# A top-k mask with the subtraction turned round, and a weight decode with its passes in another order

## The chip, the cores and the metric

The kernel runs on one core of one Trainium2 chip. The metric is the device time of one execution in microseconds. Before the change it is 1667.4 us, the median of three runs (1666.01 to 1667.79).

The core has five engines that run side by side and meet through semaphores: TensorE (PE, with weight loads shown as PEld), VectorE (DVE), ScalarE (ACT), GpSimd (POOL) and SyncE (SP), which here only issues DMAs. Each engine takes its instructions strictly in order, so an instruction that waits holds up everything behind it on that engine.

## The reference

Attention with a top-32 mask per query row, then a feed-forward block with an ELU.

```python
# q, k, v: (8, 8, 576, 64) float32
scores = scale * np.matmul(q, k.transpose(0, 1, 3, 2))
kth = np.partition(scores, -32, axis=-1)[..., -32:-31]
scores = np.where(scores >= kth, scores, -1e9)
scores = scores - np.max(scores, axis=-1, keepdims=True)
attn = np.exp(scores)
attn = attn / (np.sum(attn, axis=-1, keepdims=True) + 1e-09)
x = np.matmul(attn, v)                       # then (B,H,S,D) -> (4608, 512)
h = x @ w_in                                 # w_in  (512, 2048)
g = np.where(h > 0, h, np.exp(np.minimum(h, 0)) - 1)
out = g @ w_out                              # w_out (2048, 512)
```

The two weight matrices arrive as 64-bit floats. The kernel reads each weight as two 32-bit words and puts a 32-bit float together from them on the chip.

## The kernel before, in words

**Attention steps.** The queries are cut into tiles of 128 rows (and a rest of 64 per image). One `Step` is one tile with one pair of heads; there are 144. Per step, PE computes the scores of both heads into PSUM (`scores`, L299), ACT copies them to the tile `sc` (L307), and DVE finds the 32 largest values of each row: four rounds of an eight-wide maximum with a replace between them. The 32nd largest is the last column of `u.last` (`low` in `mask`), the largest the first column of `u.first` (`top`).

**Mask.** `mask(u, i)` takes one head of a step. POOL forms `neg = -low` (L366) and `gap = low - top` (L368), both 128x1. ACT then runs a leaky rectifier with bias `neg` in place (L369): scores from the 32nd up become `s - low`, the others are multiplied by 1e30. A second pass, the exponential with bias `gap` (L370), turns the kept ones into exp(s - top) and the others into 0, and adds up the row for the denominator. Then POOL forms the reciprocal and scales both heads (`normalise`, L380 to L387), PE transposes the result (`turn`, L406), ACT copies it out (L407), PE multiplies it with v (`attend`, L432) and ACT copies that to `xT` (L459).

**Feed-forward pieces.** `feed` hands out pieces of the feed-forward block between the parts of a step: `hidden` (PE L504, ACT L514, L517 and L519, DVE L476 for the ELU) and `project` (PE L529). A piece is only handed out once `decoded` says that the weights it needs have been through the decode.

**Decode.** There are 32 weight pieces of 128x512, 16 of `w_in` and 16 of `w_out`. `load_weight` brings one into a `raw` tile (SP queue, L153); `raw` has seven buffers. In that tile the low word (`lo`) and the high word (`hi`) of each weight alternate, so each is read and written at a stride of 8 bytes; `sign` is the top byte of the low word. `convert_first(i)` runs on ACT a Copy that scales the low word (L174), a Sign that writes the byte (L175) and an Abs that scales the high word in place (L178), and on POOL a clamp of the high word (L179). `convert_last(i)` shifts the high word on DVE (L186) and adds both words on POOL into the final weight tile (L187). `decode_piece(i)` does `convert_first(i)` and `convert_last(i - 3)`; it is called by `hook`, which the rounds of the selection call. Each of the first eight steps calls it four times, always in pairs, and step 8 three times, 35 calls in all.

**Order.** The first eight steps (`n < tight`) use `select_row` and `mask(cur, i)` on the step itself, and outside the first few lines of the start-up the order of instructions on each engine is worked out by the scheduler of the framework. From step 8 on the order is the written one: step n selects, while step n-1 is masked and step n-2 transposed.

Of the kernel before, what the change touches and what calls it, by code (L numbers as in the profile page):

```python
# [8 lines left out]
AF = mybir.ActivationFunctionType  # L9
ALU = mybir.AluOpType  # L10
FP32 = mybir.dt.float32
U32 = mybir.dt.uint32
I32 = mybir.dt.int32
# [3 lines left out]
TOP_K = 32  # L17
TAKEN = -1.0e30
EPS = 1.0e-9
STEEP = 1.0e30  # L20
HIDDEN = {1: 1.1, 2: 1.85, 3: 2.7}
PROJECT = 3.55

# [58 lines left out]
def kernel(  # L82
# [9 lines left out]
    nc = tc.nc  # L92
    P = nc.NUM_PARTITIONS
# [8 lines left out]
    NF = dff // P  # L102
# [3 lines left out]
    scale = 1.0 / float(D) ** 0.5  # L106
# [3 lines left out]
    def pool(name, bufs, **kw):  # L110
        return ctx.enter_context(tc.tile_pool(name=name, bufs=bufs, **kw))
# [7 lines left out]
    small = pool("small", 4)  # L119
# [20 lines left out]
    raw = {}  # L140

    def weight(i):
        per = dff // WN
        if i < NC * per:
            f, c = divmod(i, NC)
            src = moe_w_in[c * P : (c + 1) * P, 2 * f * WN : 2 * (f + 1) * WN]
            return src, w_in[:, c, f * WN : (f + 1) * WN]
        f = i - NC * per
        return moe_w_out[f * P : (f + 1) * P, :], w_out[:, f, :]

    def load_weight(i):
        t = rawpool.tile([P, 2 * WN], U32, tag="raw", name="raw")
        nc.sync.dma_start(t[:], weight(i)[0])  # L153
        raw[i] = t

    def parts(t):
        words = t[:].rearrange("p (n w) -> p n w", w=2)
        signs = t[:].bitcast(FP8).rearrange("p (n w) -> p n w", w=8)
        return words[:, :, 0], words[:, :, 1], signs[:, :, 3]

    def convert_first(i):

        lo, hi, sign = parts(raw[i])
        ef, mf = hi.bitcast(FP32), lo.bitcast(FP32)
        nc.scalar.activation(mf, lo, AF.Copy, scale=2.0**-35, bias=2.0**17)  # L174
        nc.scalar.activation(  # L175
            sign, ef, AF.Sign, scale=2.0**64, bias=1.0, saturate=False
        )
        nc.scalar.activation(ef, ef, AF.Abs, scale=2.0**-62)  # L178
        nc.gpsimd.tensor_scalar(  # L179
            ef, ef, (2.0 - 2.0**-3 - 2.0**-23) * 2.0**-46, 2.0**-77, ALU.min, ALU.max  # L180
        )

    def convert_last(i):
        t, dst = raw.pop(i), weight(i)[1]
        lo, hi, sign = parts(t)
        nc.vector.tensor_single_scalar(hi, hi, 3, ALU.logical_shift_left)  # L186
        nc.gpsimd.tensor_tensor(  # L187
            dst.bitcast(I32), hi.bitcast(I32), lo.bitcast(I32), ALU.add
        )

    decode = []
    decoded = [0]
# [10 lines left out]
            late["x"] = ctx.enter_context(tc.tile_pool(name="xt", bufs=2))  # L203

    def decode_piece(i):
        if i < 2 * NF:
            if i + 3 < 2 * NF:
                load_weight(i + 3)
            convert_first(i)
        if i > 2:  # L210
            convert_last(i - 3)
            decoded[0] = i - 2

    loaded, kqT, vT = {}, {}, {}

# [65 lines left out]
    def turn_qk(whole=False):  # L281
        while turning:
            if next(turning[0], turning) is turning:
                turning.pop(0)
            elif not whole:
                return
# [3 lines left out]
    def scores(u):  # L290

        u.sc = scpool.tile([P, 2, S], FP32, tag="sc", name="sc")
        q0 = QUERIES + u.t.qt * P
        for half in range(2):
            for h, i, rows in u.heads:
                kq = kqT[u.t.b, h // 2]
                part = slice(i * D, (i + 1) * D)
                k0 = (KEYS if i == 0 else 0) + half * HS
                nc.tensor.matmul(  # L299
                    wide[i][rows, half, 0:HS],  # L300
                    kq[part, q0 : q0 + u.t.ql],
                    kq[part, k0 : k0 + HS],
                    start=True,
                    stop=True,
                )
        for i in range(2):
            nc.scalar.activation(  # L307
                u.sc[:, i, :].rearrange("p (a s) -> p a s", a=2),
                wide[i][:, :, 0:HS], AF.Copy, scale=scale,
            )  # L310

    def select_row(u, i):
        if i == 0:
            u.first = small.tile([P, 2, 8], FP32, tag="m1", name="m1")
            u.last = small.tile([P, 2, 8], FP32, tag="m4", name="m4")
        sc = u.sc[:, i, :]
        m = u.first[:, i, :]
        nc.vector.max(m, sc)
        wk = wkpool.tile([P, S], FP32, tag=f"wk{i}", name="wk")
        cur = sc  # L320
        for r in range(TOP_K // 8 - 1):
            nc.vector.match_replace(wk[:], m, cur, TAKEN)
            cur = wk[:]
            if r < TOP_K // 8 - 2:
                m = small.tile([P, 8], FP32, tag=f"m{i}", name="m")[:]
            else:
                m = u.last[:, i, :]
            nc.vector.max(m, cur)
            if r > 0:
                hook()  # L330
            if r != 1:
                yield
# [21 lines left out]
            hook()  # L354
            yield

    def mask(u, i):

        if u.masked:
            return  # L360
        if i == 0:
            u.den = small.tile([P, 2], FP32, tag="den", name="den")
        u.masked = i == 1
        sc, low, top = u.sc[:, i, :], u.last[:, i, 7:8], u.first[:, i, 0:1]
        neg = small.tile([P, 1], FP32, tag="neg", name="neg")
        nc.gpsimd.tensor_scalar_mul(neg[:], low, -1.0)  # L366
        gap = small.tile([P, 1], FP32, tag="gap", name="gap")
        nc.gpsimd.tensor_tensor(gap[:], low, top, ALU.subtract)  # L368
        nc.scalar.activation(sc, sc, AF.Prelu, bias=neg[:], alpha=STEEP)  # L369
        nc.scalar.activation(  # L370
            sc, sc, AF.Exp, bias=gap[:], accum_out=u.den[:, i : i + 1]
        )

    def normalise(u):

        if u.normal:
            return
        u.normal = True
        den = small.tile([P, 2], FP32, tag="dene", name="dene")
        nc.gpsimd.tensor_scalar_add(den[:], u.den[:], EPS)  # L380
        rec = small.tile([P, 2], FP32, tag="rec", name="rec")
        nc.gpsimd.tensor_tensor(rec[:], den[:], power[:], ALU.pow)
        nc.gpsimd.tensor_tensor(den[:], den[:], rec[:], ALU.mult)
        nc.gpsimd.tensor_scalar(den[:], den[:], -1.0, 2.0, ALU.mult, ALU.add)
        nc.gpsimd.tensor_tensor(rec[:], rec[:], den[:], ALU.mult)
        for i in range(2):
            nc.gpsimd.tensor_scalar(  # L387
                u.sc[:, i, :], u.sc[:, i, :], rec[:, i : i + 1], 1.0, ALU.mult, ALU.mult
            )
# [168 lines left out]
    for b in range(B):  # L558
# [12 lines left out]
        for qt in range(J + 1):  # L571
# [8 lines left out]
            t = Tile(b, qt, rows, blk, slice(c0, c0 + n))  # L580
# [72 lines left out]
    def step(n):  # L653
        return steps[n] if 0 <= n < NS else None
# [3 lines left out]
    for n in range(NS + 3):  # L658
        for fn, args in todo.pop(n, []):
            fn(*args)  # L660
        ahead, cur, prev, done = step(n + 2), step(n), step(n - 1), step(n - 2)
        if n < tight:
            turn_qk(True)
            scores(ahead)
            for i in range(2):
                passes = select_row(cur, i)
                next(passes)
                if i == 0:
                    while closing:
                        attend(closing.pop(0))  # L670
                elif prev:
                    normalise(prev)
                    turn(prev, main)
                    turn(prev, rest)
                    turn(prev, other)
                feed(n, 0.25)
                next(passes)
                mask(cur, i)
                feed(n, 0.25)
            continue  # L680
        if n == tight:
            ctx.enter_context(tc.manual_schedule(engines=engines))
        passes = select(cur) if cur else iter(range(4))
        if ahead:
            scores(ahead)
        while closing:
            attend(closing.pop(0))
        next(passes)
        feed(n, 0.25)
        if prev:  # L690
            mask(prev, 0)
        turn_qk()
        next(passes)
        feed(n, 0.25)
        if done:
            turn(done, main)
            turn(done, rest)
        if prev:
            mask(prev, 1)
        next(passes)  # L700
        feed(n, 0.25)
        if done:
            turn(done, other)
        next(passes)
        if prev:
            normalise(prev)
        feed(n, 0.25)
        turn_qk(True)
# [36 lines left out]
```

## Time and profile before

| what | value |
|---|---|
| median of three runs | 1667.4 us |
| the profiled execution | 1667.02 us, its span 1665.2 us |
| PE busy | 1592.8 us, 96% of the span |
| DVE busy | 1495.8 us, 90% |
| ACT busy | 1165.1 us, 70% |
| POOL busy | 630.5 us, 38% |
| mean granted TensorE clock | 0.977 |

The shares are averages over parts of the run that differ. The decode falls into the first 150 us. In the 40 slices of the page, of 41.6 us each, PE is busy 5, 5, 8 and then 9 tenths for the rest, and the granted clock of TensorE reads 9, 5, 7, 8 and then 9. DVE's busy share falls off only in the last three slices.

### The profile page before, as it was taken

The numbers are of one execution on the slowest core, as the hardware profiler recorded it, in microseconds if no ns is written. First come the engines' busy times: TensorE is split into PE (matmuls) and PEld (weight loads), VectorE is DVE, ScalarE is ACT, GpSimd is POOL, SyncE is SP. The second block draws the span as 40 slices with busy tenths as digits, with TensorE's granted clock in tenths as the row PEclk, the third lists the DMA queues.
The fourth block names the chain that finished last, engine by engine and source line by source line (L and its number), as shares of the span: only waits on it lengthen the run. The fifth ranks groups of instructions, "written<-read, shape, count | busy, mean of one in ns | idle before, by whom it ended". The sixth has DMA issues, their size and how long they took to land.

```text
span 1665.2 us, 25986 instructions
## 1 busy us (share of the span) xinstructions
PE 1592.8 (96%) x8528; PEld 1031.5 (62%) x8528; DVE 1495.8 (90%) x3044; ACT 1165.1 (70%) x2377; POOL 630.5 (38%) x1719
## 2 busy tenths in 40 slices
PE   5589999999999999999999999999999999999999
PEld 3366677657574767656566676755557575755565
DVE  5887999999999999999999999999999999998500
ACT  6998777668686777678667685868758585857521
POOL 3775444333334334333334333333333343332200
PEclk9578999999999999999999999999999999999999
DMA  7540120001100110001100111001200100000000
GB/s 211 171 144 7 23 50 29 7 15 44 48 1 8 43 42 22 1 28 37 42 14 1 50 29 35 1 14 43 50 13 1 28 15 29 7 7 7 7 13 13
DMA packets 101126, 56.21 MB, mean 34 GB/s; under 512 B 84096, under 2 KB 92288, under 8 KB 100992
## 3 DMA queue, kind: packets, MB, share of 16 engines
q1 hardware_dynamic: 99792, 54.26, 11.7%
q8 instruction: 68, 1.11, 0.3%
q14 instruction: 66, 0.54, 0.1%
q10 hardware_dynamic: 1200, 0.30, 0.1%
HBM read 45.09 MB, written 9.44 MB: 33 GB/s over the span
## 4 chain that ended last, share of the span: by engine, by line
PE 65%; DVE 21%; ACT 9%; POOL 3%; issue 2%; SPq 0%; DMA 0%; ACTq 0%; POOLq 0%; DVEq 0%
PE ops L529 24%; PE hps L504 20%; DVE wk L346 9%; DVE m L353 8%; PE avps L432 7%; PE scps L299 6%; PE eps L406 5%; DVE m L341 3%; ACT sc L370 2%; ACT sc L369 1%; DVE gT L476 1%; ACT raw L175 1%; PE qkps L269 1%; ACT et L407 1%; POOL w_in L187 1%
## 5 line engine op out<-in xcount | busy, mean ns | idle before, releaser
L353 DVE MAX8 m<-wk 128x8 f32<-128x576 f32 x816 | 577.0, 750 | 0.0
L504 PE MATMUL hps<-xT,w_in 128*128 128x256 f32 (+2 forms) x2432 | 548.1, 374 | 12.5 <-ACT xT L459 12.3
L529 PE MATMUL ops<-w_out,gT 128*128 128x512 f32 x1152 | 522.8, 598 | 0.0
L504 PEld LDWEIGHTS hps<-xT,w_in 128*128 128x128 f32 x2432 | 406.5, 193 | 109.2 <-issue 23.8
L346 DVE MATCH_REPLACE8 wk<-m,wk 128x576 f32<-128x576 f32 x544 | 400.8, 746 | 0.0
L529 PEld LDWEIGHTS ops<-w_out,gT 128*128 128x128 f32 x1152 | 208.7, 190 | 233.0 <-issue 219.5
L380 POOL TENSOR_SCALAR dene<-den 128x2 f32<-128x2 f32 x144 | 35.9, 249 | 771.2 <-ACT sc L370 770.6
L369 ACT ACTIVATE sc<-sc,neg 128x576 f32<-128x576 f32 x288 | 226.8, 788 | 89.2 <-POOL neg L366 89.0
L370 ACT ACTIVATE sc<-sc,gap 128x576 f32<-128x576 f32 x288 | 224.1, 778 | 25.7 <-ACT sc L369 0.7
L387 POOL TENSOR_SCALAR sc<-sc,rec 128x576 f32<-128x576 f32 x288 | 221.0, 778 | 14.9
L307 ACT ACTIVATE sc<-scps 128x576 f32<-128x576 f32 x288 | 174.0, 659 | 73.3 <-PE scps L299 73.3
L299 PE MATMUL scps<-kqT 64*128 64x288 f32 (+1 forms) x1280 | 201.8, 440 | 21.2 <-ACT kqT L275 7.9
L407 ACT COPY et<-eps 128x512 f32<-128x512 f32 x288 | 166.8, 579 | 55.2 <-PE eps L406 55.0
L346 DVE MATCH_REPLACE8 wk<-m,sc 128x576 f32<-128x576 f32 x272 | 200.4, 746 | 0.0
L432 PE MATMUL avps<-et,vT 128*64 128x256 f32 (+2 forms) x2080 | 193.3, 326 | 4.8 <-ACT et L407 4.6
L406 PEld LDWEIGHTS eps<-ident,sc 128*128 128x128 f32 x1152 | 143.6, 144 | 83.8 <-issue 46.2
L476 DVE SCALAR_TENSOR_TENSOR gT<-n,gT 128x512 f32<-128x512 f32 (+1 forms) x132 | 100.2, 759 | 102.0 <-ACT n L519 101.9
L341 DVE MAX8 m<-sc 128x8 f32<-128x576 f32 x272 | 191.8, 748 | 0.0
L406 PE MATMUL eps<-ident,sc 128*128 128x128 f32 x1152 | 175.7, 278 | 15.4 <-POOL sc L387 13.0
L432 PEld LDWEIGHTS avps<-et,vT 128*64 128x64 f32 x2080 | 122.6, 141 | 79.1 <-issue 22.8
L299 PEld LDWEIGHTS scps<-kqT 64*128 64x128 f32 (+1 forms) x1280 | 108.1, 181 | 91.9 <-issue 44.2
L514 ACT ACTIVATE n<-hps 128x512 f32<-128x512 f32 (+1 forms) x156 | 88.0, 564 | 71.4 <-PE hps L504 67.5
(47 smaller groups left out, 1170.2 us busy)
## 6 DMA issues: line engine op xcount, KB each, us to landing
kin<-in_k_dram SPq DMA_DIRECT2D x64, 128.0 KB, 2.8
raw<-in_moe_w_in_dram SPq DMA_DIRECT2D x16, 512.0 KB, 5.4
vT<-in_v_dram SPq DMA_DIRECT2D x64, 128.0 KB, 2.3
raw<-in_moe_w_out_dram SPq DMA_DIRECT2D x16, 512.0 KB, 3.9
out_dram<-osb SPq DMA_DIRECT2D x32, 256.0 KB, 2.3
qin<-in_q_dram SPq DMA_DIRECT2D x62, 128.0 KB, 2.8
kin<-in_k_dram SPq DMA_DIRECT2D x32, 32.0 KB, 2.4
vT<-in_v_dram SPq DMA_DIRECT2D x64, 16.0 KB, 2.2
```

The costliest lines, as they stand in the source:

```text
L299: nc.tensor.matmul(wide[i][rows, half, 0:HS], kq[part, q0 : q0 + u.t.ql], kq[part, k0 : k0 + HS], start=True, stop=True,)
L341: nc.vector.max(found[i], cur[i])
L346: nc.vector.match_replace(wk[i], found[i], cur[i], TAKEN)
L353: nc.vector.max(found[i], cur[i])
L369: nc.scalar.activation(sc, sc, AF.Prelu, bias=neg[:], alpha=STEEP)
L370: nc.scalar.activation(sc, sc, AF.Exp, bias=gap[:], accum_out=u.den[:, i : i + 1])
L387: nc.gpsimd.tensor_scalar(u.sc[:, i, :], u.sc[:, i, :], rec[:, i : i + 1], 1.0, ALU.mult, ALU.mult)
L406: nc.tensor.transpose(ps[:, c * P : (c + 1) * P], sc[:, c0 : c0 + P], ident[:])
L407: nc.scalar.copy(g.et[:, chunks, u.at, :], ps[:, 0 : n * P].rearrange("p (c q) -> p c q", c=n),)
L432: nc.tensor.matmul(ps[i * D : (i + 1) * D, cols], vt[:, 2 * J + i if c == J else i * J + c, :], w, start=(c == 0), stop=(c == J),)
L504: nc.tensor.matmul(blk.h[:, f % bank, :], w_in[:, i, f * P : (f + 1) * P], blk.xT[:, i, 0:n_tok], start=(i == 0), stop=(i == NC - 1),)
L529: nc.tensor.matmul(blk.o[:], blk.gT[f // NG][:, f % NG, s * P : (s + 1) * P], w_out[:, f, :], start=(f == 0), stop=(f == NF - 1),)
```

## The change

Five edits:

1. `mask` no longer forms `neg`. The rectifier gets scale -1 and bias `low`, so that it works on `low - s`: the scores that fall out stay as they are, the kept ones are multiplied by 2^-96. The exponential gets scale -2^96, which undoes that for the kept ones and sends the others to 0.
2. `gap` is formed on DVE in the first eight steps and on POOL after that, as before.
3. Of the three ACT passes of a weight piece, Abs comes first and writes into the final weight tile instead of in place; Copy follows.
4. The POOL clamp (now in the final tile) and the Sign pass move one call of `decode_piece` later.
5. The DVE shift works in the final tile, one call earlier than before relative to the last add; the add is in place in the final tile.

```diff
-STEEP = 1.0e30
+STEEP = 2.0**96
...
-        lo, hi, sign = parts(raw[i])
-        ef, mf = hi.bitcast(FP32), lo.bitcast(FP32)
-        nc.scalar.activation(mf, lo, AF.Copy, scale=2.0**-35, bias=2.0**17)
+        lo, hi, _ = parts(raw[i])
+        nc.scalar.activation(weight(i)[1], hi.bitcast(FP32), AF.Abs, scale=2.0**-62)
+        nc.scalar.activation(lo.bitcast(FP32), lo, AF.Copy, scale=2.0**-35, bias=2.0**17)
+
+    def convert_second(i):
+        _, hi, sign = parts(raw[i])
+        w = weight(i)[1]
+        nc.gpsimd.tensor_scalar(
+            w, w, (2.0 - 2.0**-3 - 2.0**-23) * 2.0**-46, 2.0**-77, ALU.min, ALU.max
+        )
         nc.scalar.activation(
-            sign, ef, AF.Sign, scale=2.0**64, bias=1.0, saturate=False
+            sign, hi.bitcast(FP32), AF.Sign, scale=2.0**64, bias=1.0, saturate=False
         )
-        nc.scalar.activation(ef, ef, AF.Abs, scale=2.0**-62)
-        nc.gpsimd.tensor_scalar(
-            ef, ef, (2.0 - 2.0**-3 - 2.0**-23) * 2.0**-46, 2.0**-77, ALU.min, ALU.max
-        )
+
+    def convert_third(i):
+        w = weight(i)[1].bitcast(U32)
+        nc.vector.tensor_single_scalar(w, w, 3, ALU.logical_shift_left)
 
     def convert_last(i):
-        t, dst = raw.pop(i), weight(i)[1]
-        lo, hi, sign = parts(t)
-        nc.vector.tensor_single_scalar(hi, hi, 3, ALU.logical_shift_left)
-        nc.gpsimd.tensor_tensor(
-            dst.bitcast(I32), hi.bitcast(I32), lo.bitcast(I32), ALU.add
-        )
+        w, t = weight(i)[1].bitcast(I32), raw.pop(i)
+        nc.gpsimd.tensor_tensor(w, w, parts(t)[0].bitcast(I32), ALU.add)
...
     def decode_piece(i):
-        if i < 2 * NF:
-            if i + 3 < 2 * NF:
-                load_weight(i + 3)
-            convert_first(i)
-        if i > 2:
-            convert_last(i - 3)
-            decoded[0] = i - 2
+        stages = (convert_first, convert_second, convert_third, convert_last)
+        if i + 3 < 2 * NF:
+            load_weight(i + 3)
+        for ago, stage in enumerate(stages):
+            if 0 <= i - ago < 2 * NF:
+                stage(i - ago)
+        decoded[0] = max(0, i - 2)
...
-    def mask(u, i):
+    def mask(u, i, engine=nc.gpsimd):
...
-        neg = small.tile([P, 1], FP32, tag="neg", name="neg")
-        nc.gpsimd.tensor_scalar_mul(neg[:], low, -1.0)
         gap = small.tile([P, 1], FP32, tag="gap", name="gap")
-        nc.gpsimd.tensor_tensor(gap[:], low, top, ALU.subtract)
-        nc.scalar.activation(sc, sc, AF.Prelu, bias=neg[:], alpha=STEEP)
+        engine.tensor_tensor(gap[:], low, top, ALU.subtract)
+        nc.scalar.activation(sc, sc, AF.Prelu, scale=-1.0, bias=low, alpha=1.0 / STEEP)
         nc.scalar.activation(
-            sc, sc, AF.Exp, bias=gap[:], accum_out=u.den[:, i : i + 1]
+            sc, sc, AF.Exp, scale=-STEEP, bias=gap[:], accum_out=u.den[:, i : i + 1]
         )
...
-                mask(cur, i)
+                mask(cur, i, nc.vector)
```

## The prediction

> **What bounds the kernel now.** I read four views in this order: the busy time by stretch of the span, the groups of ACT in the decode, ACT's instructions in order of time there, and the list of who waited for whom. The columns of the first are the stretch, its length, then busy time (and instructions) of PE, PEld, DVE, ACT and POOL, the granted clock, the DMA share and GB/s.
>
> ```profile
> 13.00:40.00 27.00, 20.59 (x100) 13.86 (x96) 21.43 (x45) 21.32 (x40) 9.17 (x22) 0.94 0.75 227
> 40.00:145.00 105.00, 71.69 (x355) 52.76 (x356) 78.78 (x162) 103.02 (x175) 74.05 (x124) 0.66 0.41 126
> 145.00:300.00 155.00, 152.94 (x1192) 110.72 (x1191) 155.00 (x321) 111.74 (x238) 65.37 (x184) 1.00 0.11 29
> 300.00:600.00 300.00, 289.25 (x1568) 195.19 (x1567) 300.00 (x615) 220.01 (x459) 114.83 (x331) 1.00 0.10 26
> 600.00:1666.00 1066.00, 1055.58 (x5309) 656.67 (x5307) 940.12 (x1903) 704.03 (x1460) 364.73 (x1048) 1.00 0.08 21
> ```
>
> There are three stages with three limits. From 40 to 145 us ACT is busy 103.0 of 105.0 us while PE and DVE have 33 and 26 us to spare: ACT sets the pace. From 145 to 600 us DVE has no idle time at all (455.00 of 455). After 600 us PE is busy 1055.6 of 1066. Each stage hands over to the next, and the orders are fixed, so a microsecond saved in the first stage moves the end by about one. A microsecond saved on POOL or ACT after 145 us is worth nothing unless DVE or PE waited for it.
>
> What fills ACT in the first stage (13 to 145 us):
>
> ```profile
> L175 ACT ACTIVATE raw<-raw 128x512 fp8e4<-128x512 f32 x31 | 39.8, 1418 | 0.1
> L178 ACT ACTIVATE raw<-raw 128x512 f32<-128x512 f32 x31 | 20.6, 737 | 0.1
> L174 ACT ACTIVATE raw<-raw 128x512 f32<-128x512 uint32 x31 | 20.4, 731 | 0.7 <-DMA raw<-in_moe_w_in_dram 0.7
> L307 ACT ACTIVATE sc<-scps 128x576 f32<-128x576 f32 x22 | 14.6, 683 | 4.4 <-PE scps L299 4.4
> ```
>
> The decode is 80.8 us of ACT. Sign alone is half: its mean is 1418 ns against 731 and 737. The change keeps all three passes, so the bulk stays. The question is what of ACT's order and of its waits changes. ACT in order of time (start, length, line; in brackets the idle time before it and who ended it):
>
> ```profile
> 9.33 1.33 ACT L175 ACTIVATE raw<-raw 128x512 fp8e4<-128x512 f32 x1
> 10.42 0.35 ACT L261 COPY kqT<-scps 128x128 f32<-128x128 f32 x1
> ...
> 13.75 1.34 ACT L175 ACTIVATE raw<-raw 128x512 fp8e4<-128x512 f32 x1
> ...
> 15.67 1.17 ACT L307 ACTIVATE sc<-scps 128x576 f32<-128x576 f32 x2
> ...
> 83.02 2.51 ACT L175 ACTIVATE raw<-raw 128x512 fp8e4<-128x512 f32 x2
> 85.24 1.31 ACT L178 ACTIVATE raw<-raw 128x512 f32<-128x512 f32 x2
> 86.40 0.80 ACT L369 ACTIVATE sc<-sc,neg 128x576 f32<-128x576 f32 x1
> 87.82 0.58 ACT L407 COPY et<-eps 128x512 f32<-128x512 f32 x1 [0.63 <-PE eps L406]
> ...
> 104.89 0.71 ACT L519 ACTIVATE n<-n 128x512 f32<-128x512 f32 x1
> 105.41 1.34 ACT L174 ACTIVATE raw<-raw 128x512 f32<-128x512 uint32 x2
> ```
>
> ACT runs one pass right behind another. Of the instructions that end an idle time from 40 us on, only three are over a tenth: 0.70 (at 57.9), 0.65 (at 72.9) and 0.63 us, all the copy of the transposed scores, which waits for PE, which waits for POOL's scaling. The whole run's waits say the same of the mask:
>
> ```profile
> ACT sc L369 <- POOL neg L366: 89.0, 72, 4.5
> POOL neg L366 <- DVE m L353: 63.1, 80, 3.0
> DVE raw L186 <- POOL raw L179: 38.3, 19, 12.2
> ```
>
> The rectifier's wait of 89 us looks large, but most of it is a wait for the selection itself (POOL's `neg` waits 63 us for DVE's last maximum), and nearly all falls after 145 us, where ACT is idle a fourth of the time. It isn't 89 us to be had.
>
> **The change part by part.**
>
> The mask. Removed: 288 POOL instructions `neg`, median 0.22 us, 63 us of POOL. POOL is busy 38%, so that buys nothing by itself. ACT's two passes stay at 0.8 us each: scale and alpha are numbers in the instruction and both biases were pointers before. After 145 us each rectifier starts up to 0.3 us earlier (0.22 and the hop). Who gains? DVE waits for nothing until 600 us. PE's waits for ACT after 600 us add up to 5.6 us in 12 places (2.4 scores, 1.3 and 0.6 the transposed copy, 1.3 keys), and 0.3 us in some of them makes 0 to 3 us; I take 0.5, since the mask precedes few of them. In the first stage the wait for `neg` never stops ACT between 13 and 145 us (idle 0.0 at L369): nothing.
>
> The 16 `gap` on DVE: no row shows it there. Lower bound the 0.07 us of DVE's 128x8 value load, upper bound the 0.19 us of the same subtraction on POOL: 1.1 to 3.0 us of DVE. I take 1.1, the row of the same engine. It is covered by the 26 us that DVE idles in the first stage; without that cover it would cost its own length. The exponential then waits for DVE instead of POOL, right behind the last maximum, ahead of whatever DVE does next.
>
> Abs into the final tile. Read at a stride of 8 bytes, written densely. Bounds: 0.58 us from start to start as now (1.18 for the pair at 85.24), or 0.52 as the dense L519 at 104.89 has it. Times 32: 0 to 2 us saved; I take 1.0, half way, as one of two sides becomes dense. The same on POOL (clamp 0.66, add 1.04) and DVE (shift 0.43) is off the path, since these wait for ACT, not ACT for them.
>
> A rule speaks against that 1.0. The Trainium skill's page "SBUF — State Buffer" (the note on cachelines in "Door 1: The DMA port swizzle") holds that a stride of up to 16 bytes runs at full bandwidth, and "GPSIMD Engine Reference", "Performance pitfalls for Q7 kernels", that GpSimd pays only above 8 bytes. By these dense writing is worth 0 and the sum below would be 4.4 instead of 5.4. The rows at 85.24 and 104.89 leave a gap of 0.06 us, but between two functions, so they don't refute it.
>
> Abs first. In each pair ACT now runs Copy, Copy, Sign, Sign, Abs, Abs; POOL's clamp, then DVE's shift and POOL's add wait for the last. With Abs ahead the clamp is released some 3.5 us sooner (1.13 + 2.22 from the starts 81.9, 83.0 and 85.2). POOL is in order: clamp, shift, add and then the chain of `normalise` follow. With `neg` and `gap` gone from it as well (0.4 us a head), the scaling ends sooner and the three waits at L407 shrink: 0 to 2.0 us, I take 1.3, two of the three.
>
> Sign a call later. (a) At the start, piece 1's Sign (13.75, 1.37 us to the next) stands ahead of the score copy at 15.67, and the chain of waits runs through both; piece 0's (1.09 us) stands ahead of the copies at 10.42. ACT idles 2.37 us before 26.7 and 2.02 before 34.0, room for both. 0 if the scheduler puts them back in the same place, 2.4 if both go; I take 1.4, the one that the chain shows. (b) At the end of the stage DVE leaves its wait for the ELU at 138.5 and is the bound from there. One Sign fewer lies ahead of that point, 1.2 us (half of 2.22, with what follows): 0 to 1.2, I take 1.2. (c) Its price: the last Sign, piece 31, now falls into step 8, whose order is the written one, behind two score copies:
>
> ```profile
> 148.63 1.04 POOL L187 TENSOR_TENSOR w_out<-raw 128x512 int32<-128x512 int32 x1 [2.07 <-DVE raw L186]
> 149.76 0.23 POOL L380 TENSOR_SCALAR dene<-den 128x2 f32<-128x2 f32 x1
> 149.75 1.19 ACT L307 ACTIVATE sc<-scps 128x576 f32<-128x576 f32 x2 [4.08 <-PE scps L299]
> ```
>
> ACT would end it at 149.75 + 1.19 + 1.2, about 152.1, so POOL's last add starts 3.5 us later than 148.63, and `normalise` behind it too; PE's transposes at 153.1 wait about as long. PE idles 12.8 us between 145 and 600 (155.00 - 152.94 and 300 - 289.25), and DVE needs nothing of it: I price it at 0, and at 3.5 us if PE's spare time is needed elsewhere.
>
> No DMA is added or dropped: the load of piece i+3 stands at the head of the same call, and a `raw` buffer comes free with the same add.
>
> Sum: 0.5 + 1.0 + 1.3 + 1.4 + 1.2 = 5.4 us. The profiled execution took 1667.02 (span 1665.2 and 1.8 around it), so 1661.6; from the median of 1667.4 it is 1662.0. I say 1662.
>
> **The rivals.**
>
> *Nothing moves (chance 0.18).* ACT's work is the same, and the waits that vanish come back elsewhere, as an engine that is 98% busy has only 2.0 us to give after 40 us. For it: that 2.0, and a scheduler that may keep the order. Against: the Signs on the early chain. Time: only terms of 0.5 and 1.0 remain, 1665.9.
>
> *The decode's tail gets longer (0.24).* Place: POOL's add, which now waits for a Sign that ACT runs behind the next pieces' Abs and Copy. In call i the add of piece i-3 follows a Sign two calls old instead of three. From the point on where POOL reaches the add before ACT is through that Sign, `normalise` behind it is late, and ACT itself waits at L407. Price: up to 1.2 us (one Sign) in half of the eight steps, 4.8 us, and the 3.5 us of step 8 not absorbed, less the 1.4 and 0.5 that still hold: 6.4 us slower, 1673.4. For it: POOL is busy 74 of 105 us and starts `normalise` within 0.1 us of the add (83.82 to 83.90). Against: the clamp is released 3.5 us sooner, which pays for a Sign.
>
> *More than the sum (part of the forecast's 0.58).* All upper ends: 3 + 2 + 2 + 2.4 + 1.2 = 10.6, so 1656.4.
>
> **How the numbers follow.** Under 0.2%, some 3.3 us, a measurement of this kernel can't tell a difference from none. The forecast's own range is 1656 to 1664, the second case lies at 1663 to 1668, the third at 1667 to 1675. Faster gets 0.58 from the first and 0.02 from the second, 0.60; same gets 0.16 of the second and 0.02 of the third's edge, 0.18; slower 0.22. For 8 in 10 the range goes from 1656, the upper ends together, to 1670, the middle of the third case.
>
> **What would show it.** Right: ACT's idle times at L407 between 40 and 145 us gone; the first Signs later than the score copy that now starts at 15.67; DVE's first step without ACT waits starting near 134 instead of 138.5; the clamp no longer waiting 33.7 us for Abs; everything after that shifted by the same few us. POOL should lose 63 us, without effect. Wrong: ACT with new idle times in the first stage, POOL's add waiting for ACT, or a DVE that idles after 145 us.

## The result, and the profile after

| | median | runs | ratio to before |
|---|---|---|---|
| before | 1667.41 us | 1665.69 to 1667.89 (12) | |
| after | 1664.2 us | 1662.89 to 1667.1 (12) | 0.9982, 95% interval 0.9975 to 0.999 |

The change makes the kernel faster by 0.18%, some 3 us: at the edge of what can be told from no change; a second set of runs gave the same ratio (1664.52 us, 0.9982, 0.9973 to 0.999). The forecast was 1662.0, so 5.4 us were expected.

One profiled execution must be read with care here. That of the changed kernel took 1666.29 us, 2.1 above its median, so it shows 0.7 us of the 3. A second one, taken with the experiments, took 1664.20 (span 1662.4). Both are used below. In both, the difference to before is there within the first 160 us and only drifts after that: the first output copy ends 0.9 us earlier in the one and 3.0 in the other, the last one 0.7 and 2.9.

Busy time by stretch of the changed kernel, first profile (stretch, length, then PE, PEld, DVE, ACT, POOL, granted clock, DMA share, GB/s):

```profile
13.00:40.00 27.00, 18.24 (x72) 11.58 (x68) 20.35 (x45) 17.69 (x35) 7.39 (x15) 0.87 0.73 218
40.00:145.00 105.00, 74.42 (x386) 53.96 (x386) 90.85 (x182) 104.81 (x180) 75.70 (x99) 0.71 0.40 129
145.00:300.00 155.00, 153.28 (x1197) 111.03 (x1195) 155.00 (x319) 113.29 (x239) 58.81 (x153) 1.00 0.11 29
```

ACT is still full from 40 to 145 us, 104.8 of 105. The new thing is DVE, 90.9 us there instead of 78.8, though the only work added to it is 16 small subtractions. POOL has not become lighter in this stretch (75.7 against 74.1) in spite of 25 instructions fewer. Before 40 us ACT does 3.6 us less than it did.

ACT's groups from 13 to 145 us (line, engine, operation, out<-in, number; then busy us, mean ns of one, idle time before them and what ended it):

```profile
L182 ACT ACTIVATE raw<-raw 128x512 fp8e4<-128x512 f32 x31 | 44.9, 1448 | 0.1
L174 ACT ACTIVATE raw<-raw 128x512 f32<-128x512 uint32 x31 | 23.7, 766 | 0.0
L310 ACT ACTIVATE sc<-scps 128x576 f32<-128x576 f32 x22 | 15.4, 719 | 7.3 <-PE scps L302 7.3
```

Sign into single bytes is still the largest; the 7.3 us of idle time at the score copy are looked at next. The start, on ACT (start, length, line; in brackets the idle time before it):

```profile
15.00 1.34 ACT L182 ACTIVATE raw<-raw 128x512 fp8e4<-128x512 f32 x1
16.09 1.26 ACT L310 ACTIVATE sc<-scps 128x576 f32<-128x576 f32 x2
...
37.01 1.19 ACT L310 ACTIVATE sc<-scps 128x576 f32<-128x576 f32 x2 [4.54 <-PE scps L302]
...
40.73 0.66 ACT L173 ACTIVATE w_in<-raw 128x512 f32<-128x512 f32 x1
```

and on PE:

```profile
34.06 0.69 PE L412 MATMUL eps<-ident,sc 128*128 128x128 f32 x2 [5.19 <-POOL sc L393]
34.68 2.29 PE L302 MATMUL scps<-kqT 64*128 64x288 f32 x8
```

The Sign of piece 1 still stands ahead of the score copy (15.00, then 16.09). And there is a new wait that no line of the diff asks for: the scheduler now puts two transposes of step 0 ahead of the scores of a later step. PE stands 5.2 us for POOL's scaling, ACT 4.5 us for PE, and the decode of piece 3 begins at 40.7 us, where it was 36.7.

Two places on DVE, the add that POOL ran beside the first of them, and the point where DVE leaves its last wait for ACT (the hand-over):

```profile
99.94 1.54 POOL L192 TENSOR_TENSOR w_out<-w_out,raw 128x512 int32<-128x512 int32 x1
100.23 1.27 DVE L374 TENSOR_TENSOR gap<-m,m 128x1 f32<-128x1 f32 x1
...
118.57 1.53 DVE L188 TENSOR_SCALAR w_out<-w_out 128x512 uint32<-128x512 uint32 x1
...
137.46 0.69 DVE L482 SCALAR_TENSOR_TENSOR gT<-n,gT 128x512 f32<-128x512 f32 x1 [2.11 <-ACT n L525]
```

A subtraction of 128x1, 0.15 us in the median, took 1.27 while POOL's add ran, and a shift of 0.43 took 1.53 beside the next add. That is where most of DVE's 12 busy us more come from: from 40 to 145 us the subtractions take 7.9 us, 29 shifts 16.1 (27 took 13.5 before) and the ELU's four instructions 3.7 instead of 2.7. The hand-over stood at 138.53 before, stands at 137.46 here, and in the second profile of the same kernel at

```profile
135.48 0.69 DVE L482 SCALAR_TENSOR_TENSOR gT<-n,gT 128x512 f32<-128x512 f32 x1 [2.08 <-ACT n L525]
```

### The profile page after: what moved, and what is told of

It is laid out like the page before. It is cut to its first block, busy times and chain, and to the rows that moved or that the text cites. A ratio compares the mean times of both kernels' runs of the same rounds, so it can differ in the third digit from the quotient of the medians.

```text
span 1664.5 us, 25650 instructions
## 1 busy us (share of the span) xinstructions
PE 1594.5 (96%) x8528; PEld 1031.1 (62%) x8528; DVE 1504.3 (90%) x3060; ACT 1162.7 (70%) x2377; POOL 576.6 (35%) x1415
## 4 chain that ended last, share of the span: by engine, by line
PE 60%; DVE 30%; ACT 7%; issue 2%; SPq 0%; DMA 0%; POOL 0%; DVEq 0%; ACTq 0%
PE ops L535 21%; PE hps L510 20%; DVE wk L349 13%; DVE m L356 11%; PE avps L438 6%; PE scps L302 6%; PE eps L412 5%; DVE m L344 4%; DVE gT L482 1%; ACT raw L182 1%; ACT sc L376 1%; PE qkps L272 1%; ACT raw L174 1%; ACT sc L375 1%; ACT sc L310 1%
## 5 line engine op out<-in xcount | busy, mean ns | idle before, releaser
L510 PE MATMUL hps<-xT,w_in 128*128 128x256 f32 (+2 forms) x2432 | 547.8, 374 | 12.3 <-ACT xT L465 10.2
L375 ACT ACTIVATE sc<-sc,m 128x576 f32<-128x576 f32 x288 | 227.6, 791 | 39.2 <-DVE m L356 39.0
```

Source lines behind the costliest of these rows:

```text
L375: nc.scalar.activation(sc, sc, AF.Prelu, scale=-1.0, bias=low, alpha=1.0 / STEEP)
L510: nc.tensor.matmul(blk.h[:, f % bank, :], w_in[:, i, f * P : (f + 1) * P], blk.xT[:, i, 0:n_tok], start=(i == 0), stop=(i == NC - 1),)
```

## The experiments

Each ratio is against the kernel before, run on the same chip in the same set. The first four kernels take the change apart. "The order" of an engine is that in which its instructions start in the trace, up to 145 us.

**The mask alone, gap left on POOL** (edit on the kernel before):

```diff
-        nc.gpsimd.tensor_scalar_mul(neg[:], low, -1.0)
...
-        nc.scalar.activation(sc, sc, AF.Prelu, bias=neg[:], alpha=STEEP)
+        nc.scalar.activation(sc, sc, AF.Prelu, scale=-1.0, bias=low, alpha=1.0 / STEEP)
...
```

> Only the mask is changed (no neg, subtraction turned round, gap stays on POOL everywhere); the decode is the old one. Theory A, the gain comes out of the decode's stage: nothing beyond 0.5 us, since the wait for neg never stops ACT before 145 us; ratio to before 0.9993 to 1.0003. Theory B, the gain comes from the mask (63 us less of POOL, the rectifier 0.3 us earlier): the whole 3 us, ratio about 0.9982.

Measured: 1666.06 us, ratio 0.9991 (0.9982 to 1.0). The middle of the interval is half of the gain; its ends are Theory B's full 3 us and nothing, so Theory A's range isn't excluded by this kernel. PE, ACT and DVE run the same order as before, and so does POOL but for `neg`. The hand-over on DVE comes 1.5 us earlier (136.99 instead of 138.53).

**The decode alone** (the changed kernel with the old mask, neg and gap on POOL):

> Only the decode is changed; the mask is the old one with neg and gap on POOL. Theory A: nearly the whole gain, 2 to 3.5 us, ratio 0.998 to 0.999. Theory B: nothing, ratio 1.000. If POOL's neg in the first stage hinders the new order of the decode, it is 1 to 2 us slower than with both.

Measured: 1670.11 us, ratio 1.001 (1.0001 to 1.0019). Alone the new decode is a loss of 1.7 us, barely clear of nothing. Theory A's 0.998 to 0.999 is excluded.

**The changed kernel with gap on POOL:**

```diff
-                mask(cur, i, nc.vector)
+                mask(cur, i)
```

> The changed kernel with gap on POOL in the first eight steps too. In the profile of the changed kernel gap on DVE takes up to 1.27 us where POOL works beside it. If these waits of DVE set the pace: 1 to 2 us faster than the changed kernel, 1662 to 1663. If ACT alone does: the same as the changed kernel within 0.5 us, 1664.

Measured: 1666.49 us, ratio 0.9996 (0.9987 to 1.0004). Neither: by the ratios moving gap back costs 2.3 us, with intervals that barely overlap. The waits from 13 to 145 us, here (engine and line, what it waited for, us in total, times, longest):

```profile
POOL gap L374 <- DVE m L331: 16.9, 10, 4.7
DVE w_in L188 <- POOL w_in L179: 17.5, 8, 6.1
DVE w_out L188 <- POOL w_out L179: 11.9, 8, 4.0
```

and in the changed kernel:

```profile
DVE w_in L188 <- POOL w_in L179: 14.4, 7, 5.4
DVE w_out L188 <- POOL w_out L179: 4.8, 2, 2.9
```

DVE's wait for the clamp is 29.4 us here and 19.2 there. On PE, ACT and SP the instructions of this kernel stand in the same order as in the changed one, but on DVE and POOL they don't: beside `gap` itself, shifts, clamps and adds change places with rounds of the selection. So the price of gap's place is not separated from that of the new order.

Against the decode alone this kernel only lacks `neg`, and there the order of every engine is the same. By the ratios it is 2.3 us faster (in one set, 1665.68 to 1668.5 against 1667.57 to 1670.41). But neither DVE's wait for the clamp (29.0 us in the decode alone) nor the hand-over (139.40 there, 139.78 here) shows that gain; the first output copy starts 0.7 us earlier and the last one 1.9.

**The changed kernel with Sign back in the first call:**

```diff
         nc.scalar.activation(lo.bitcast(FP32), lo, AF.Copy, scale=2.0**-35, bias=2.0**17)
+        nc.scalar.activation(
+            sign, hi.bitcast(FP32), AF.Sign, scale=2.0**64, bias=1.0, saturate=False
+        )
...
```

> The changed kernel with Sign put back into the first call, behind Abs and Copy; the rest stays. If the later Sign takes 1.2 us off ACT ahead of the point where DVE becomes the bound: 1.2 us slower than the changed kernel, about 1665.4. If ACT's order within the decode does not matter: 1664 to 1664.5.

Measured: 1668.1 us, ratio 1.0003 (0.9994 to 1.0012). By the ratios the later call is worth 3.5 us, more than was expected; the order of PE, ACT, DVE and POOL moves with it, so part may be that.

After these, and the two kernels on ACT's load below, Theory A was given up. Theory C in its place: the first stage is a loop through POOL's queue. DVE's shift waits for POOL's clamp. The clamp stands in POOL's queue behind whatever POOL does for the mask and for `normalise`, and these wait for DVE's last maximum and ACT's exponential. What leaves that queue lets DVE go on earlier. The missing cell is **the whole mask on the old decode** (edit on the mask alone):

```diff
-                mask(cur, i)
+                mask(cur, i, nc.vector)
```

> The whole change of the mask (neg gone, gap on DVE in the first eight steps) on the old decode. Theory C: the first stage is held by a loop through POOL's queue (last maximum, exponential, normalise, clamp, shift, DVE again), not by ACT's load, so each instruction that leaves POOL's queue counts, and the new decode gives nothing: 1664 to 1665, the same as the changed kernel. Theory A, ACT's order in the decode: no better than the mask without gap on DVE, 1666.

Measured: 1664.23 us, ratio 0.9982 (0.9973 to 0.9991): exactly the changed kernel (0.9982 again in a second set, 1664.52 us). The mask is the whole gain; on top of it the new decode is worth 0, to within some 2 us. The waits from 13 to 145 us fit Theory C. Before:

```profile
DVE raw L186 <- POOL raw L179: 26.2, 18, 4.0
...
POOL neg L366 <- DVE m L328: 10.7, 8, 3.1
```

The mask alone, gap on POOL:

```profile
DVE raw L186 <- POOL raw L179: 20.1, 16, 4.0
...
POOL gap L366 <- DVE m L328: 12.0, 8, 3.1
```

The whole mask, on the old decode:

```profile
DVE raw L186 <- POOL raw L179: 17.4, 16, 4.0
```

Of the 26.2 us before, 3.9 are one wait at 16.5 us; in the other two kernels that same wait (4.4 and 4.0) is put down to a DMA. Without it DVE's wait for the clamp goes 22.3, 20.1, 17.4 as the time falls by 0, 1.5 and 3 us. And POOL's own wait for the last maximum, 8 times with the clamps queued behind it, is only gone in the third: with no mask instruction left on POOL, nothing there waits for DVE's last maximum. One sees the clamp behind that wait in POOL's order of time. With gap on POOL:

```profile
63.46 0.19 POOL L366 TENSOR_TENSOR gap<-m,m 128x1 f32<-128x1 f32 x1 [2.40 <-DVE m L328]
63.74 1.63 POOL L179 TENSOR_SCALAR raw<-raw 128x512 f32<-128x512 f32 x2
```

Three things limit this. From the mask alone to the whole mask the order on DVE and POOL changes too, as above. The hand-over, 136.99 in the mask alone, stands at 137.33 with the whole mask, in an execution 0.9 us above its median: gap's share does not show there. And ACT's waits at the copies of the transposes fall as well, from 2.2 us before to 1.0 with the mask alone and 0.2 with the whole mask. With the mask alone they are

```profile
57.13 0.59 ACT L405 COPY et<-eps 128x512 f32<-128x512 f32 x1 [0.53 <-PE eps L404]
71.75 0.59 ACT L405 COPY et<-eps 128x512 f32<-128x512 f32 x1 [0.31 <-PE eps L404]
86.26 0.59 ACT L405 COPY et<-eps 128x512 f32<-128x512 f32 x1 [0.18 <-PE eps L404]
```

So an earlier scaling on POOL that reaches ACT over PE's transposes is a rival: it fits these times as the loop through DVE does, and the two are not separated.

**Is ACT's load the bound of the first stage?** Two kernels take some of it away. One puts the sign of every second piece in on DVE:

```diff
...
+        if i % 2:
...
+            nc.vector.scalar_tensor_tensor(
+                out=lo, in0=hi, scalar=0x80000000, in1=lo,
+                op0=ALU.bitwise_and, op1=ALU.bitwise_or,
+            )
+            return
```

> The changed kernel with the sign of every second piece put in by DVE (one instruction: the top bit of the high word or-ed into the low word) instead of ACT's Sign; the Copy's constants are moved so that the byte is right already. Takes 16 x 1.09 = 17.4 us off ACT and puts 16 x 0.6 = 9.6 us on DVE. If ACT is the bound of the first stage and each microsecond there moves the end by one: DVE (busy 91 of 105 us, and 10 more) becomes the bound after some 8 us are won, 1654 to 1659. If the first stage is held by POOL's chain instead: 0 to 2 us.

Measured: 1664.78 us, ratio 0.9985 (0.9976 to 0.9993). The other writes whole words, and its weights lack the sign:

```diff
-            sign, hi.bitcast(FP32), AF.Sign, scale=2.0**64, bias=1.0, saturate=False
+            hi.bitcast(FP32), hi.bitcast(FP32), AF.Sign, scale=2.0**64, bias=1.0
```

> The changed kernel with Sign writing whole 32-bit words over the high word instead of one byte of the low word, so that the sign is left out of the weights. If the byte store is what makes Sign twice as long as Abs and Copy: 0.57 us instead of 1.09 from start to start, 32 x 0.52 = 16.6 us off ACT; the end moves by 10 to 17 us if ACT is the only bound of the first stage, by less where POOL (75.7 of 105 us) and DVE take over. If Sign is slow by itself: the same as the changed kernel.

Measured: 1666.33 us, ratio 0.9995 (0.9986 to 1.0004), by the ratios even 2.2 us above the changed kernel. Busy time of the first, then of the second:

```profile
40.00:145.00 105.00, 78.89 (x385) 56.41 (x385) 93.86 (x193) 91.23 (x165) 81.92 (x99) 0.67 0.40 125
40.00:145.00 105.00, 74.68 (x368) 54.31 (x364) 83.31 (x179) 88.97 (x177) 72.63 (x98) 0.64 0.39 125
```

and ACT's groups of the second, from 13 to 145 us:

```profile
L182 ACT ACTIVATE raw<-raw 128x512 f32<-128x512 f32 x31 | 21.4, 692 | 0.0
```

The output of one byte, an fp8 value, is what doubles Sign: 692 ns in the mean when it writes words, 1448 in the changed kernel. But ACT loses 13.6 us of busy time in the first, for 3 more on DVE and 6 more on POOL, and the end does not move; it loses 15.8 in the second, where DVE and POOL are less busy as well, and the end is no earlier either. ACT's 98% was not a bound in the sense that a microsecond less there is a microsecond less at the end: where ACT has time, PE waits 22.2 and 25.7 us for POOL's scaling (9.7 in the changed kernel), and ACT for PE.

**The clamp on DVE:**

```diff
-        nc.gpsimd.tensor_scalar(
+        nc.vector.tensor_scalar(
```

> The changed kernel with the clamp on DVE instead of POOL: DVE then waits for ACT alone, and POOL loses 32 x 0.61 = 19.5 us, while DVE gains 32 x 0.33 = 10.6 us. Theory C (loop through POOL): DVE's waits for POOL, 19 us in the changed kernel, vanish, 2 to 5 us faster than the changed kernel, 1659 to 1662. Theory D (DVE with its waits for the port it shares with POOL is the bound of the first stage, 93 of 105 us busy): 3 to 8 us slower, 1667 to 1672.

Measured: 1666.15 us, ratio 0.9991 (0.9983 to 1.0), 1.5 us above the changed kernel by the ratios, with intervals that overlap. Both theories are partly right:

```profile
40.00:145.00 105.00, 73.26 (x383) 52.78 (x380) 104.62 (x210) 103.92 (x178) 57.55 (x70) 0.71 0.39 127
```

DVE's waits for POOL are gone, but now DVE too is full, 104.6 of 105. The loop is cut; that DVE's load takes its place is argued from this row, not tried.

**The reciprocal on DVE in the first eight steps:**

```diff
+        if fast:
+            nc.vector.tensor_scalar_add(den[:], u.den[:], EPS)
+            nc.vector.reciprocal(rec[:], den[:])
...
```

> The changed kernel with the reciprocal of normalise on DVE in the first eight steps: two DVE instructions of about 0.1 us instead of five on POOL of 2.3 us from start to the scaling. Theory C: 1 to 4 us faster than the changed kernel, 1660 to 1663. Theory D, or a DVE that now waits for the exponential in its own queue: the same or up to 5 us slower.

Measured: 1663.83 us, ratio 0.9978 (0.9968 to 0.9987). In the direction of Theory C, but inside the changed kernel's interval. POOL's scaling now waits 10.9 us for DVE's reciprocal, and the end is no later: a wait of POOL for DVE need not cost its length.

**PE's order of the first two steps as written:**

```diff
+            order = ExitStack()
+            if n < 2:
+                order.enter_context(tc.manual_schedule(engines={E.PE}))
...
```

> The changed kernel with PE's order in steps 0 and 1 as written. With the change the scheduler puts two transposes of step 0 ahead of the next scores; PE waits 5.2 us there for POOL's scaling and ACT 4.5 us for the scores, and the decode of piece 3 starts at 40.7 us instead of 36.7. If this idle time of ACT is on the path, since ACT is the bound from there on: 2 to 4 us faster than the changed kernel, 1660 to 1662. If the start is covered by something else: the same within 0.5 us.

Measured: 1663.18 us, ratio 0.9973 (0.9963 to 0.9983), 1.5 us better than the changed kernel beside it in the same set; the intervals overlap. The order on ACT and DVE moves with PE's. PE's longest wait falls from 10.2 to 4.1 us, and the granted clock of the stretch rises from 0.71 to 0.90:

```profile
40.00:145.00 105.00, 81.93 (x385) 58.99 (x384) 93.39 (x184) 103.03 (x176) 75.74 (x100) 0.90 0.39 126
```

**Both together:**

> The changed kernel with PE's order in steps 0 and 1 as written and the reciprocal of normalise on DVE in the first eight steps: the two that each moved the changed kernel down (ratio 0.9973 and 0.9978, against 0.9982). If the start-up wait and POOL's queue are separate costs, they add: 0.9969, about 1662.2. If both ease the same chain: 0.9973, as with the order alone.

Measured: 1661.73 us (1660.92 to 1662.98), ratio 0.9964 (0.995 to 0.9977): the best kernel of the study, twice the gain of the change itself. The interval holds both forecasts, 0.9969 and 0.9973, so whether the two gains add is not decided. From 40 to 145 us:

```profile
40.00:145.00 105.00, 84.42 (x392) 59.35 (x394) 89.97 (x194) 101.95 (x176) 65.65 (x70) 0.92 0.39 126
```

POOL has gone from 75.7 to 65.7 us there, and ACT is no longer full.

## Why the prediction came out as it did

The direction and the stage were right; 3 us came instead of 5.4. The 1664.2 lies inside the range given for 8 in 10 (1656 to 1670), 0.2 us outside the forecast's own (1656 to 1664) and inside that of *Nothing moves* (1663 to 1668). That it came so near is in part luck: the mask, priced at nothing in this stage, gave the gain, and the new decode, which stood for 4.9 of the 5.4, gave none on top of it. Only the 1.3 of *Abs first* had counted on `neg` and `gap` leaving POOL as well.

*"In the first stage the wait for neg never stops ACT between 13 and 145 us (idle 0.0 at L369): nothing."* This is the step that failed. The observation is true, the conclusion is not. `neg` and `gap` stopped POOL, not ACT: POOL stood 10.7 us for DVE's last maximum, with the clamps behind it that DVE in turn waited for. The prediction had said of these instructions that taking them off POOL "buys nothing by itself", since POOL is busy 38%. A queue's busy share does not tell what stands behind its waits. By the ratios neg is worth 1.5 us on the old decode and 2.3 on the new one, and gap's place 1.5 and 2.3; one such difference has an uncertainty of about its own size.

How far the loop explains this is shown in part, and the way over PE's transposes to ACT stands beside it. With neg gone from the old decode no order changes, DVE's wait for the clamp falls by 2.2 us and the hand-over comes 1.5 us earlier. With gap gone from POOL in the new decode that wait falls by 10 us and the hand-over comes 2.3 us earlier, but DVE's and POOL's order changes too. With neg gone from the new decode neither moves, and how those 2.3 us come about is open. So is the 3.5 us of the kernel with Sign in the first call, where DVE waits 18.5 us for the clamp, no longer than in the changed kernel.

*The 16 gaps on DVE, 1.1.* They took 8.3 us in the changed kernel and 5.0 on the old decode, far above the upper bound of 3.0, as some wait for POOL. The cover by DVE's idle time held: the end came earlier all the same.

*"A microsecond saved in the first stage moves the end by about one."* The hand-over part holds: what was won or lost by 160 us was mostly still there at the end. What does not hold is that ACT's load sets the length of that stage; 13.6 us of it could be taken away without moving the end. The signs that the prediction named for being wrong were there: ACT idles 7.3 us at the score copy (4.4 before), and POOL's adds wait 10.4 us for ACT's Sign.

*Abs into the final tile, 1.0.* The passes start 0.56 to 0.60 us apart in the pairs (49.84, 50.44, 51.00 in one), as before (0.57 to 0.59). Worth 0, as the prediction had it by the note on cachelines in the Trainium skill's "SBUF — State Buffer" ("Door 1: The DMA port swizzle"). What the step left out is that POOL's add became longer: median 1.30 us instead of 1.04, 8 us of POOL in this stage, against 1.5 us less for the clamps (0.61 instead of 0.66). It called these "off the path" as it had called neg worthless; what the longer adds cost was not tried.

*Abs first, 1.3.* The waits at the copies of the transposes went from 2.2 to 0.3 us, and DVE's for the clamp got shorter, but not by this edit: with the decode alone the first are 2.6 us and the second, from 40 us on, 25.0 (22.3 before), while the mask on the old decode already brings them to 0.2 and 17.4. What the term had counted on `neg` and `gap` came; what it had counted on Abs did not, and a start-up wait of ACT came with the new decode (4.5 us).

*Sign a call later, 1.4 and 1.2.* (a) failed: the scheduler left the early Signs where they were. (b) can't be sized: the kernel with Sign in the first call is 3.5 us slower by the ratios, but the order on PE, ACT, DVE and POOL differs too. (c), the price in step 8, did come as a wait, and cost nothing:

```profile
145.82 1.29 POOL L192 TENSOR_TENSOR w_out<-w_out,raw 128x512 int32<-128x512 int32 x1 [2.15 <-ACT raw L182]
147.17 0.22 POOL L386 TENSOR_SCALAR dene<-den 128x2 f32<-128x2 f32 x1
```

The add waits 2.15 us for Sign, and is still 2.8 us earlier than the 148.63 of before.

*After 145 us, 0.5.* Not seen from before to after: the lead of the first output copy, 0.9 and 3.0 us, is 0.7 and 2.9 at the last. From the decode alone to the kernel without neg it does grow, from 0.7 to 1.9 us.

The four decode terms, 4.9 us together, measured 0 on top of the mask, and a loss of 1.7 with the old one. Which of their parts help and which cost is not separated: with PE's order as written the kernel is 1.5 us faster, within overlapping intervals, and the longer adds were not tried alone. The rival of a longer tail did not come as described: POOL's adds do wait for Signs (10.4 us in the stage), but on top of the new mask the whole is not slower.

Two slips in the working changed nothing: the second rival's 1673.4 starts from the profiled 1667.0 and not from the forecast's 1667.4, and ACT is idle about a third of the time after 145 us, not a fourth.

## What to carry to other kernels

Before an instruction on a lightly loaded engine is priced at nothing, look at what it waits for and what stands behind it in that engine's queue: a 128x1 subtraction that waits for the end of a selection holds up every piece of unrelated work behind it. An engine that is 98% busy need not be the bound when three engines feed one another in order; take some work from it before building a sum on it. Where a scheduler orders the instructions, compare the order on all engines before and after an edit: here it moved two PE transposes far from the edit and put a wait of 5 us into the start, and moving a 128x1 subtraction to DVE reordered the shifts, clamps and adds around it.

## What the runs showed of the hardware

- An ACT pass over 128x512 that stores single bytes (fp8 values) at a stride of 8 bytes took 1448 ns in the mean, the same pass storing 32-bit words at that stride 692. Whether the type or the width does it was not tried.
- POOL's 32-bit add of 128x512 took 1.04 us with both operands at a stride of 8 bytes in one tile, and 1.30 in place with one operand dense and the other strided. Which of the two differences does it was not tried.
- Tiny DVE instructions are held up by POOL: the 128x1 subtraction took 0.136 us at the least and 1.27 at the most. In the changed kernel the five that took 1.24 us and more began inside an add of POOL, and each ended 0.02 us after it; beside POOL's 128x2 instructions of `normalise` it took 0.14 to 0.17. The Trainium skill's "SBUF — State Buffer" ("Who interferes with whom") states that a DVE instruction with two SBUF inputs contends with a GpSimd one that reads SBUF. This trace agrees beside the adds, and shows no wait beside the 128x2 ones.
- A granted clock of 0.90 instead of 0.71 over 105 us went along with a gain of only 1.5 us, in a stage where PE was busy 74.4 and 81.9 of the 105.
